# Issuing a pair's split, bits and spreading DMAs at the head of its period in a hashed attention and mixture-of-experts kernel

## The chip, the cores and the metric

The kernel runs on one NeuronCore of one Trainium2 chip. The metric is the device time of one execution in microseconds (us), the median of several runs. An execution profiled by the hardware gives the trace from which all rows below are read.

## The reference

Attention with a hash mask, then a mixture of eight experts of which each token uses one. Shapes: batch 4, 8 heads, 768 positions, head size 64; 3072 tokens of width 512 in the second part.

```python
q_bits = (einsum('bhsd,dk->bhsk', q, proj) > 0)      # 6 bits, and the same for k
mask = q_bucket[:, :, :, None] == k_bucket[:, :, None, :]
scores = where(mask, scale * q @ k.T, -1e9)
attn = softmax(scores)                               # + 1e-9 in the denominator
x = (attn @ v), heads side by side                   # 3072 x 512
e = argmax(x @ w_gate); gate = softmax(x @ w_gate)[e] * sigmoid(x @ w_output_gate)[e]
out = gate * relu(x @ w1[e]) @ w2[e]
```

## The kernel before

The first 480 us are attention, the rest experts; the change touches the attention alone. Two heads make a **pair** (16 pairs, `g`), and each pair takes 12 **steps** (`s`), one for a block of 128 queries of one head j. A step is a row of work on four engines: `scores(s)` on TensorE (PE, four matmuls into one of two `ps_s` buffers), `sc` on VectorE (DVE, line 533, reads `ps_s` and so frees it), `soft(s)` on ScalarE (ACT, the exponential, line 541), `normal` for two steps at a time (DVE: `rsum`, lines 548 and 549; GpSimd, POOL: two multiplications by it, line 551), and six steps later `transposed` (PE, line 562, and the ACT copies of line 563). Every sixth step (`k == 0`, k is s mod 6) has a **block of weighted sums** on PE (line 573, 12 matmuls in both heads) with its copy to `ot` on DVE (line 576) and the transposition `xb` (line 585). So the attention is a chain of **half periods** of six steps, each with one block; a pair has a first and a second half. In the trace a half period is read from the start of one block to that of the next.

Beside this, each pair g from 2 on is prepared one pair ahead, from step s0 = 12 (g - 1) on:

- `load(g)`: the two `qk` tiles from HBM, at step s0 - 5.
- `project(g)`: four matmuls behind the block at s0 (line 407), then the hash bits `bt` on DVE (line 410).
- `split_hi(g, j)`: the rounded part `xl` of head j, POOL, line 487, at s0 + 1 and s0 + 3.
- `split_lo(g, j, n)`: the rest `yl`, two halves for each head, DVE, line 495, at s0 + 3 to s0 + 6.
- `spread(g, j)`: eight DMAs in on-chip memory issued by the SP queue (lines 504 to 512), which place `xl`, `yl` and the bits in the operands of `scores`; at s0 + 4 and s0 + 6. The last two of them, line 512, put the query bits into `yl`.

The first step that uses all this for head 0 is s0 + 12, for head 1 it is s0 + 13. `xl`, `yl`, `xr` and `yr` have four buffers, so a pair's tiles take the place of those of two pairs before. In three of the pairs (steps 72, 120, 168) the DVE also works on the router's gate around s0 (lines 661 to 665 and 198 to 220, at step 168 with lines 767 to 776).

PE, DVE, ACT and POOL run in the order in which the code is written: the functions planned by `plan(step, ...)` come at the end of a step, those in `narrow` beside the block. The SP queue's order is set by a scheduler instead, and it is served strictly from the front: a DMA that waits holds all behind it.

## Time and profile before

| what | value |
|---|---|
| median of 3 runs | 816.14 us (815.57 to 816.91) |
| the profiled execution | 818.71 us, its span 816.9 us |
| PE busy | 767.9 us, 94% of the span |
| DVE, ACT, POOL busy | 489.1, 461.0 and 382.4 us |
| mean granted clock of PE | 0.971 of full speed |

Busy time is over the whole span; in a stretch of it another engine can be the one that is waited for. The 1.8 us between the profiled execution's time and its span lie outside the trace.

### The profile page before, as it was taken

To read this page: it belongs to the slowest core of one execution; us is meant where nothing else is said; L and a number is where in the kernel's file an instruction comes from. 1 tells how busy PE (TensorE), PEld (TensorE's weight loads), DVE (VectorE), ACT (ScalarE), POOL (GpSimd) and SP (SyncE) were. 2 spreads that over 40 slices of the span, in tenths; PEclk is the share of its full clock that TensorE was granted. 3 is DMA by queue.
4 is the path that set the end of the run, shared out by engine and by line. 5 is a ranking of instruction groups with operands and counts; after the bars stand their busy time and mean duration, and the time that the engine had idled before them with its cause. 6 is when DMAs were issued, how large, how long until landed. Compare 5 with 4: busy or idle time off the path is not lost. (4 is left out here: it accounts for less than half of the span.)

```text
span 816.9 us, 13705 instructions
## 1 busy us (share of the span) xinstructions
PE 767.9 (94%) x4690; PEld 619.9 (76%) x4690; DVE 489.1 (60%) x1032; ACT 461.0 (56%) x934; POOL 382.4 (47%) x422
## 2 busy tenths in 40 slices
PE   7999898999898999898998999979999999999997
PEld 5767566767656767667667767878899999998895
DVE  6778575788575788576777654434636354464740
ACT  6787575777675777676776873124333424253431
POOL 7456353444353444353435885443526463737201
PEclk8999998999998999999999999999999999999999
DMA  5545344456244455245345423435443545445511
GB/s 170 131 105 132 92 99 124 103 122 153 52 99 121 105 122 141 64 100 135 92 104 137 115 71 71 138 97 195 131 142 128 185 132 184 147 151 160 204 51 38
DMA packets 84798, 98.88 MB, mean 121 GB/s; under 512 B 57999, under 2 KB 59439, under 8 KB 84720
## 3 DMA queue, kind: packets, MB, share of 16 engines
q1 hardware_dynamic: 79376, 84.58, 38.9%
q0 software_dynamic: 5200, 13.31, 4.9%
q8 instruction: 40, 0.66, 0.3%
q14 instruction: 38, 0.31, 0.1%
q10 hardware_dynamic: 144, 0.02, 0.0%
HBM read 59.49 MB, written 13.11 MB: 89 GB/s over the span
## 5 line engine op out<-in xcount | busy, mean ns | idle before, releaser
L551 POOL TENSOR_SCALAR sc<-sc,rsum 128x768 f32<-128x768 f32 x192 | 176.7, 934 | 242.2 <-DVE rsum L549 146.7
L563 ACT COPY pts<-ps_t 128x384 f32<-128x384 f32 x384 | 165.8, 482 | 124.7 <-PE ps_t L562 124.3
L533 DVE TENSOR_SCALAR_CACHE_REDUCE sc<-ps_s 128x768 f32<-128x768 f32 x192 | 182.4, 954 | 79.3 <-PE ps_s L529 78.3
L541 ACT ACTIVATE sc<-sc,mn 128x768 f32<-128x768 f32 x192 | 178.7, 936 | 12.2 <-DVE sc L533 11.1
L562 PE MATMUL ps_t<-ident,sc 128*128 128x128 f32 x1152 | 168.9, 285 | 9.3 <-ACT pts L563 4.8
L562 PEld LDWEIGHTS ps_t<-ident,sc 128*128 128x128 f32 x1152 | 138.6, 146 | 45.0 <-POOL sc L551 20.9
L573 PE MATMUL ps_a<-pts,vt 128*64 128x384 f32 x768 | 131.9, 493 | 0.0
L529 PE MATMUL ps_s<-yr,yl 76*128 76x384 f32 x384 | 105.3, 357 | 23.7 <-DMA yl<-bt 23.0
L529 PE MATMUL ps_s<-xr,xl 128*128 128x384 f32 x384 | 119.6, 394 | 3.7 <-POOL xl L477 2.2
L573 PEld LDWEIGHTS ps_a<-pts,vt 128*64 128x64 f32 x768 | 52.5, 137 | 68.4 <-issue 68.2
L323 DVE SCALAR_TENSOR_TENSOR hl<-ps_s,hh 128x256 fp32r<-128x256 f32 (+8 forms) x40 | 34.0, 849 | 116.4 <-ACT hh L322 108.4
L312 PE MATMUL ps_s<-xh,w1h 128*128 128x256 f32 (+7 forms) x288 | 97.0, 337 | 0.0
L312 PE MATMUL ps_s<-xlo,w1h 128*128 128x256 f32 (+7 forms) x288 | 95.3, 331 | 0.0
L312 PE MATMUL ps_s<-xh,w1l 128*128 128x256 f32 (+7 forms) x288 | 95.1, 330 | 0.0
L529 PEld LDWEIGHTS ps_s<-yr,yl 76*128 76x128 f32 x384 | 73.8, 201 | 26.3 <-DMA xr<-xl 15.3
L286 POOL DMA_INDIRECT xq<-x_dram,idx x75 | 81.6, 1089 | 23.1 <-issue 20.5
L329 POOL DMA_INDIRECT out_dram<-yo,sid x29 | 30.5, 1052 | 123.3 <-ACT yo L328 72.3
L322 ACT ACTIVATE hh<-ps_s 128x256 fp32r<-128x256 f32 (+8 forms) x40 | 29.1, 727 | 104.3 <-PE ps_s L312 76.3
L529 PEld LDWEIGHTS ps_s<-xr,xl 128*128 128x128 f32 x384 | 61.5, 201 | 6.7 <-DVE sc L533 2.6
L312 PEld LDWEIGHTS ps_s<-xh,w1h 128*128 128x128 f32 x288 | 54.1, 188 | 2.1 <-issue 0.6
L312 PEld LDWEIGHTS ps_s<-xlo,w1h 128*128 128x128 f32 x288 | 54.1, 188 | 1.3 <-DVE xlo L269 0.2
L312 PEld LDWEIGHTS ps_s<-xh,w1l 128*128 128x128 f32 x288 | 54.1, 188 | 1.1
(204 smaller groups left out, 1034.5 us busy)
## 6 DMA issues: line engine op xcount, KB each, us to landing
w_raw<-in_w_dram SPq DMA_DIRECT2D x36, 512.0 KB
qk<-in_qkT_dram SPq DMA_DIRECT2D x32, 384.0 KB
xh<-in_w_dram SPq DMA_DIRECT2D x14, 512.0 KB
xlo<-in_w_dram SPq DMA_DIRECT2D x14, 512.0 KB
vt<-in_v_dram SPq DMA_DIRECT2D x16, 384.0 KB
xr<-xl SPq DMA_DIRECT2D x30, 192.0 KB
yr<-xl SPq DMA_DIRECT2D x30, 192.0 KB
xr<-yl SPq DMA_DIRECT2D x30, 192.0 KB
```

The costliest lines, as they stand in the source:

```text
L286: nc.gpsimd.indirect_dma_start(out=xq[:, k * P:(k + 1) * P], out_offset=None, in_=x_dram.rearrange("n (a f) -> (n a) f", a=NB32), in_offse ...
L312: nc.tensor.matmul(ps, l, r, start=first and k == 0, stop=last and k == len(pairs) - 1)
L322: nc.scalar.activation(hh, ph, AF.Relu)
L323: return lambda: nc.vector.scalar_tensor_tensor(hl, ph, 0.0, f32(hh), ALU.max, ALU.subtract)
L329: nc.gpsimd.indirect_dma_start(out=out[:, :], out_offset=bass.IndirectOffsetOnAxis(ap=sid[0:n, r, a:a + 1], axis=0), in_=yo[0:n], in_offse ...
L529: nc.tensor.matmul(ss[:, n, 0:HS], l[0:k, qs], r[0:k, n * HS:(n + 1) * HS], start=first, stop=not first)
L533: nc.vector.tensor_scalar(sc, ss[:, :, 0:HS], MASKED, None, ALU.min, ALU.min, accum_out=mn)
L541: nc.scalar.activation(pr, pr, AF.Exp, bias=mn, scale=-1.0, accum_out=sums[s // GROUP][:, k:k + 1])
L551: nc.gpsimd.tensor_scalar(live[s0 + k], live[s0 + k], rs[:, k:k + 1], 0.0, ALU.mult, ALU.add)
L562: nc.tensor.transpose(tr[:, c], pr[:, (3 * h + c) * P:(3 * h + c + 1) * P], ident)
L563: nc.scalar.copy(pts[:, 3 * h:3 * h + 3, t * P:(t + 1) * P], tr)
L573: nc.tensor.matmul(st["av"][j * D:(j + 1) * D], st["v"][:, j, c], blocks[hb][j][:, c], start=(c == 0), stop=(c == NT - 1))
```

## The change

For pairs from 2 on, the whole preparation is written at step s0 itself: both `split_hi` ahead of everything else there, the four `split_lo` in two groups behind the two `normals()` that follow the exponentials, then the block and `project`, then both `spread`. The loads come at s0 - 8. One of the six exponentials of a half period comes at k = 2 instead of k = 1. Pair 1 gets its own, slightly shifted steps. No instruction is added or removed, and no buffer changes.

```diff
--- before.py
+++ after.py
@@ -377,7 +377,7 @@
         batches = [dict() for _ in range(B)]
         blocks = {}
         sums = {}
-        at, narrow = {}, {}
+        at, first, amid, ahead, narrow, last = {}, {}, {}, {}, {}, {}
 
 
         LAG = PER
@@ -717,19 +717,21 @@
         for g in range(NP):
             s0 = 12 * (g - 1)
             if g >= 2:
-                plan(s0 - 5, lambda g=g: load(g))
+                plan(s0 - 8, lambda g=g: load(g))
+                first.setdefault(s0, []).extend(lambda g=g, j=j: split_hi(g, j) for j in range(2))
+                amid.setdefault(s0, []).extend(lambda g=g, n=n: split_lo(g, 0, n) for n in range(2))
+                ahead.setdefault(s0, []).extend(lambda g=g, n=n: split_lo(g, 1, n) for n in range(2))
+                narrow.setdefault(s0, []).append(lambda g=g: project(g))
+                last.setdefault(s0, []).extend(lambda g=g, j=j: spread(g, j) for j in range(2))
+            elif g == 1:
+                plan(4, lambda: project(1))
+                for j in range(2):
+                    plan(2 + j, lambda j=j: split_hi(1, j))
+                    for n in range(2):
+                        plan(3 + 2 * j + n, lambda j=j, n=n: split_lo(1, j, n))
+                    plan(5 + j, lambda j=j: spread(1, j))
             if g >= 1:
-                s0 += g == 1
-                if g == 1:
-                    plan(s0 + 4, lambda g=g: project(g))
-                else:
-                    narrow.setdefault(s0, []).append(lambda g=g: project(g))
                 plan(s0 + 10, lambda g=g: load_v(g))
-                for j in range(2):
-                    plan(s0 + 1 + 2 * j, lambda g=g, j=j: split_hi(g, j))
-                    for n in range(2):
-                        plan(s0 + 3 + 2 * j + n, lambda g=g, j=j, n=n: split_lo(g, j, n))
-                    plan(s0 + 4 + 2 * j, lambda g=g, j=j: spread(g, j))
             for hf in range(2 if g + 1 < NP else 1):
                 narrow.setdefault(12 * g + 6 * hf + 2 * PER, []).extend(
                     lambda hb=2 * g + hf, c=c: weighted(hb, c) for c in range(NT))
@@ -888,18 +890,23 @@
                     normals()
                     softs(1)
                 elif k == 0:
+                    for fn in first.get(s, ()):
+                        fn()
                     normals()
-                    while raw and raw[0] < s:
-                        softs(2)
-                        normals()
-                    for fn in narrow.get(s, ()):
+                    softs(2)
+                    normals()
+                    for fn in amid.get(s, ()):
                         fn()
-                    softs(1)
+                    softs(2)
+                    normals()
+                    for when in (ahead, narrow, last):
+                        for fn in when.get(s, ()):
+                            fn()
                 elif k == 3:
                     normals()
                 if s >= LAG:
                     transposed(s - LAG, live.pop(s - LAG))
-                if s >= PER and k in (1, 3):
+                if s >= PER and k in (2, 3):
                     softs(1)
                 for fn in at.get(s, ()):
                     fn()
```

On the SP queue the order of the DMAs changes with the code. Before, between the pair whose tiles are numbered below 1030 and the next one (from 1235 on); `xl`, `yl` and `bt` are sources or targets in on-chip memory:

```order
L506 DMA xr_1027<-yl_971 64x768
L507 DMA xl_920<-xl_920 64x768
L504 DMA xr_1302<-xl_1235 64x768
L512 DMA yl_971<-bt_835 12x384 x2
L505 DMA yr_1303<-xl_1235 64x768
L511 DMA yr_1303<-bt_1195 12x384 x2
```

After, the end of one pair's second `spread` (1163, 1182, 1208) and the beginning of the next pair's (1507, 1554):

```order
L512 DMA yl_1182<-bt_1205 12x384
L511 DMA yr_1208<-bt_1205 12x384
L512 DMA yl_1182<-bt_1205 12x384
L394 DMA qk_1325<-in_qkT_dram 128x768
L394 DMA qk_1327<-in_qkT_dram 128x768
L592 DMA x_dram_63<-xb_1239 32x24x32 x4
L399 DMA vt_1479<-in_v_dram 128x768
L504 DMA xr_1553<-xl_1507 64x768
L505 DMA yr_1554<-xl_1507 64x768
```

Before, the last two DMAs of a pair (line 512, `yl_971`) stand behind the next pair's line 504, which reads that pair's `xl_1235`. After, a pair's DMAs all stand ahead of the next pair's.

On DVE, from the `sc` of the step s0 (the third of the first row) to the steps after it, before:

```order
L533 TENSOR_SCALAR sc,mn<-ps_s 128x768 x3
L548 TENSOR_SCALAR rsum<-rsum 128x2
L549 RECIPROCAL rsum<-rsum 128x2
L548 TENSOR_SCALAR rsum<-rsum 128x2
L549 RECIPROCAL rsum<-rsum 128x2
L576 COPY ot<-ps_a 128x384
L410 TENSOR_SCALAR bt<-ps_m,pj 128x384
L585 STREAM_TRANSPOSE xb<-ot 128x384
L533 TENSOR_SCALAR sc,mn<-ps_s 128x768 x3
```

and after, at the same place:

```order
L533 TENSOR_SCALAR sc,mn<-ps_s 128x768 x3
L548 TENSOR_SCALAR rsum<-rsum 128x2
L549 RECIPROCAL rsum<-rsum 128x2
L495 SCALAR_TENSOR_TENSOR yl<-qk,pj,xl 128x384 x2
L548 TENSOR_SCALAR rsum<-rsum 128x2
L549 RECIPROCAL rsum<-rsum 128x2
L495 SCALAR_TENSOR_TENSOR yl<-qk,pj,xl 128x384 x2
L576 COPY ot<-ps_a 128x384
L410 TENSOR_SCALAR bt<-ps_m,pj 128x384
L585 STREAM_TRANSPOSE xb<-ot 128x384
L533 TENSOR_SCALAR sc,mn<-ps_s 128x768 x3
```

The four `split_lo` (line 495), which stood one by one between later `sc`, now all stand ahead of the `sc` of step s0 + 1. On POOL the two `split_hi` of a pair, before one by one with two multiplications of line 551 between them, now stand together ahead of those of s0:

```order
L487 TENSOR_SCALAR xl<-qk,pj 128x768 x2
L551 TENSOR_SCALAR sc<-sc,rsum 128x768 x10
```

## Rows read from the trace of the kernel before

**Rows 1.** The page's part 1: busy time of each engine, its share of the span, and the number of instructions.

```profile
PE 767.9 (94%) x4690; PEld 619.9 (76%) x4690; DVE 489.1 (60%) x1032; ACT 461.0 (56%) x934; POOL 382.4 (47%) x422
```

**Rows 2.** The view of waits, whole kernel, TensorE: who waited for whom, us in total, times, longest.

```profile
PE ps_s L529 <- DMA yl<-bt: 23.0, 7, 4.0
```

**Rows 3.** The same view for the SP queue, its largest row.

```profile
SPq L504 <- POOL xl L487: 105.9, 17, 10.1
```

**Rows 4.** The timeline at the first of these waits: start, us, engine, line, operation; in brackets the idle time before it and what ended it. The block at 83.75 us is that of step 36, and the bits in `bt` that line 512 moves are those of the pair whose scores PE is at.

```profile
82.03 1.47 SPq L507 DMA_DIRECT2D xl<-xl  x1
...
90.02 0.91 POOL L487 TENSOR_SCALAR xl<-qk,pj 128x768 fp32r<-128x768 f32 x1
90.95 0.46 SPq L504 DMA_DIRECT2D xr<-xl  x1
91.50 1.61 SPq L512 DMA_DIRECT2D yl<-bt  x2
...
93.79 0.98 PE L529 MATMUL ps_s<-yr,yl 76*128 76x384 f32 x2 [4.01 <-DMA yl<-bt]
```

**Rows 5.** Busy time by stretch, for six half periods from block to block: the stretch, its length, then busy us (and instructions) of PE, PE's weight loads, DVE, ACT and POOL, then the granted clock of PE, the share of the DMA engines and GB/s. First, second, first, second half of two pairs; a first half; and the first half from step 72, with the gate's work.

```profile
57.13:70.53 13.40, 13.40 (x93) 9.54 (x93) 9.90 (x22) 10.48 (x25) 7.97 (x12) 1.00 0.23 45
70.53:83.75 13.22, 12.68 (x86) 9.39 (x85) 10.26 (x24) 10.56 (x25) 7.46 (x22) 1.00 0.81 193
83.75:102.83 19.08, 15.07 (x93) 11.02 (x92) 9.74 (x22) 10.67 (x25) 7.49 (x13) 0.91 0.30 80
102.83:115.44 12.61, 12.61 (x86) 9.39 (x85) 9.99 (x24) 10.48 (x25) 6.38 (x7) 1.00 0.72 160
115.44:136.10 20.66, 17.30 (x102) 12.57 (x101) 10.77 (x24) 11.55 (x27) 7.66 (x8) 0.83 0.22 63
177.65:193.63 15.98, 14.92 (x105) 10.98 (x104) 14.12 (x35) 10.59 (x25) 7.74 (x8) 1.00 0.26 63
```

**Rows 6.** The timeline of the head of an undisturbed first half: the block, what DVE and POOL do beside it, the `sc` of step s0 + 1 (at 63.65), and PE's scores of step s0 + 3 (at 65.29).

```profile
57.13 4.09 PE L573 MATMUL ps_a<-pts,vt 128*64 128x384 f32 x24
57.33 0.96 DVE L533 TENSOR_SCALAR_CACHE_REDUCE sc<-ps_s 128x768 f32<-128x768 f32 x1 [0.53 <-PE ps_s L529]
...
58.21 0.16 DVE L548 TENSOR_SCALAR rsum<-rsum 128x2 f32<-128x2 f32 x1
...
58.77 1.79 POOL L551 TENSOR_SCALAR sc<-sc,rsum 128x768 f32<-128x768 f32 x2 [2.88 <-DVE rsum L549]
...
59.86 0.73 DVE L548 TENSOR_SCALAR rsum<-rsum 128x2 f32<-128x2 f32 x1 [1.28 <-ACT sc L541]
...
60.98 1.80 POOL L551 TENSOR_SCALAR sc<-sc,rsum 128x768 f32<-128x768 f32 x2 [0.42 <-DVE rsum L549]
...
61.27 0.56 DVE L576 COPY ot<-ps_a 128x384 f32<-128x384 f32 x1 [0.48 <-PE ps_a L573]
...
62.07 0.68 DVE L410 TENSOR_SCALAR bt<-ps_m,pj 128x384 fp32r<-128x384 f32 x1 [0.25 <-PE ps_m L407]
...
62.66 0.57 DVE L585 STREAM_TRANSPOSE xb<-ot 128x384 f32<-128x384 f32 x1
...
63.65 0.96 DVE L533 TENSOR_SCALAR_CACHE_REDUCE sc<-ps_s 128x768 f32<-128x768 f32 x1 [0.42 <-PE ps_s L529]
...
65.29 0.60 PE L529 MATMUL ps_s<-xr,xl 128*128 128x384 f32 x2
```

**Rows 7.** The timeline of the same half, later: two `split_lo` (line 495) on DVE beside two multiplications on POOL.

```profile
67.53 0.61 DVE L495 SCALAR_TENSOR_TENSOR yl<-qk,pj,xl 128x384 fp32r<-128x384 f32 x1
...
67.81 2.00 POOL L551 TENSOR_SCALAR sc<-sc,rsum 128x768 f32<-128x768 f32 x2 [3.24 <-PE ps_s L529]
68.06 0.95 DVE L533 TENSOR_SCALAR_CACHE_REDUCE sc<-ps_s 128x768 f32<-128x768 f32 x1
...
68.94 1.28 DVE L495 SCALAR_TENSOR_TENSOR yl<-qk,pj,xl 128x384 fp32r<-128x384 f32 x1
...
70.14 0.94 DVE L533 TENSOR_SCALAR_CACHE_REDUCE sc<-ps_s 128x768 f32<-128x768 f32 x1
```

**Rows 8.** The timeline of the first half from step 72 (block at 177.65 us): a gate operation, the `ot` copy, the `sc` of step s0 + 1, and PE's scores of step s0 + 3.

```profile
176.52 0.77 DVE L661 TENSOR_SCALAR den<-den 128x6 f32<-128x6 f32 x1
...
181.79 0.56 DVE L576 COPY ot<-ps_a 128x384 f32<-128x384 f32 x1 [1.03 <-PE ps_a L573]
...
185.58 0.94 DVE L533 TENSOR_SCALAR_CACHE_REDUCE sc<-ps_s 128x768 f32<-128x768 f32 x1
...
186.58 0.62 PE L529 MATMUL ps_s<-xr,xl 128*128 128x384 f32 x2 [0.52 <-DVE sc L533]
```

**Rows 9.** Two shorter waits of PE in the timeline, in the first halves from step 60 and from step 156, which have the same work.

```profile
162.77 0.85 PE L562 MATMUL ps_t<-ident,sc 128*128 128x128 f32 x6 [0.95 <-POOL sc L551]
...
407.36 1.12 PE L562 MATMUL ps_t<-ident,sc 128*128 128x128 f32 x6 [1.92 <-POOL xl L487]
```

**Rows 10.** These two half periods in the view by stretch, with the columns of rows 5.

```profile
149.67:164.25 14.58, 13.63 (x99) 9.93 (x96) 10.41 (x27) 10.42 (x27) 7.75 (x8) 1.00 0.27 64
393.30:409.70 16.40, 14.48 (x100) 10.60 (x96) 11.52 (x27) 11.14 (x27) 7.44 (x8) 0.94 0.31 71
```

**Rows 11.** The timeline of a second half (block at 70.53 us): a left-over `split_lo` and the wait of PE behind it.

```profile
75.76 1.21 DVE L495 SCALAR_TENSOR_TENSOR yl<-qk,pj,xl 128x384 fp32r<-128x384 f32 x1
...
79.42 0.84 PE L562 MATMUL ps_t<-ident,sc 128*128 128x128 f32 x6 [0.54 <-ACT pts L563]
```

## The prediction

> **What bounds the kernel now.** I read the busy times first: TensorE is busy 94% of the span [rows 1], so only what it waits for, or runs slowly through, can be won. The view of its waits comes next. Its one large row with a cause in the operands is a DMA: seven waits for `yl<-bt`, 23.0 us, the longest 4.0 [rows 2]. To see why these transfers are late I read the SP queue's own waits: it stood 105.9 us at line 504 for POOL's `xl` [rows 3]. The timeline joins the two [rows 4]. SP has issued line 507 by 83.5 us and then issues nothing until POOL has rounded the next pair's `xl` (90.02 to 90.93). It goes on with line 504 at 90.95 and only then with line 512, which moves bits that have been ready for half a period; PE, at the second step of this pair, starts its second product at 93.79, after 4.01 us of nothing. The reader is to see a queue served from the front: the transfer that PE needs stands behind one that belongs to the next pair. From issue to use it took under 2.3 us; what was late is the issue.
>
> The half periods give the price [rows 5]. An undisturbed first half takes 13.40 us, all of it PE busy. The disturbed one takes 19.08, 5.68 more, of which the wait is 4.01. The other 1.67 is the clock: its granted mean is 0.91, so for part of the stretch PE ran at 1.2 instead of 2.4 GHz, after the wait. A second one takes 20.66 at 0.83.
>
> **What the change removes.** In the new order of the SP queue a pair's line 512 always precedes the next pair's line 504, and both `spread` are issued a whole pair ahead. So the seven waits go: -23.0. With them goes the slow clock. For the first that is 1.67; for the second 20.66 - 13.40 - 3.4 = 3.9 (its wait, read as the mean of the seven, 23.0 / 7 = 3.3, moves this by 0.1). I take five of the first kind and two of the second, a choice: 5 x 1.7 + 2 x 3.9 = 16.3. Removed: -39.3 (all seven of the first kind would be -34.9).
>
> The half from step 156 holds a wait of 1.92 us at POOL [rows 9] and takes 16.40 where the same work takes 14.58 [rows 10]; a `split_hi` and a `split_lo` stand in that knot and go: -1.8.
>
> Second halves: 13.22 us where a `split_lo` is left over from the first half, 12.61 where none is [rows 5]; the 1.21 us of that instruction delay an exponential, then PE by 0.54 [rows 11]. No such remainder is left after the change. Against that, the exponential moved from k = 1 to k = 2 stands directly before that of k = 3, which makes ACT's copies late; I allow 0.2 us a half for it, less than half of that 0.54. About seven second halves win 0.4, seven lose 0.2: -1.4.
>
> The loads come earlier by three steps and land long before use; nothing waits for them: 0.
>
> **What it adds.** The moved work has the cover of a block (4.09 us) and of `project`. POOL's two `split_hi`, 0.91 each, fit in its 2.88 us of idle time before the first multiplication [rows 4, 6]: 0, and with that cover gone they would delay `rsum`'s readers by at most 1.8. DVE is the question, since the first `sc` after the block, that of step s0 + 1, frees the `ps_s` buffer for PE's scores of s0 + 3, and four `split_lo` now stand ahead of it. Before, DVE idles 1.28 + 0.48 + 0.25 + 0.42 = 2.4 us in this stretch, and the `sc` ends at 64.61, 0.7 before PE wants the buffer (65.29) [rows 6]. Together 3.1 us of cover against 4 x 0.61 = 2.4 [rows 7]. On these numbers the splits are free.
>
> They are not quite free, because of POOL. A `split_lo` that meets a running multiplication takes 1.28 instead of 0.61: begun at 68.94, it ends at 70.22, 0.41 after POOL's end at 69.81; and POOL's pair beside the earlier split takes 2.00 instead of 1.79 [rows 6, 7]. So the two take turns, instruction by instruction. `rsum` at 59.86 does the same: 0.73, until POOL's end. Walking the new order through the head, in us from the block's start: `rsum` 1.08, first split 1.36, POOL's first multiplication from 1.85 to 2.75, second split done 3.15, POOL's second to 4.05, second `rsum` 4.08, third split 4.15 to 4.7, POOL's third to 5.55, fourth split done 5.95, `ot` at 5.87 (before 4.14), `bt` 6.4, `xb` 7.0, `sc` from 7.5 to 8.45. PE wants the buffer at 8.16: a wait of 0.35. This walk lets an instruction start some 0.08 before the recorded end of the one ahead, as DVE does in rows 7; with full durations it gives 9.1, a wait of 1.0. I take 0.6 for each of the eleven heads without gate work: +6.6, with bounds 0 and 1.0 (11.0).
>
> The Trainium skill (GPSIMD Engine Reference, section 1, Specifications) says that POOL shares its SBUF interfaces with VectorE, with contention where a DVE instruction has two SBUF inputs or a two-port mode. `split_lo` has two such inputs, so by that rule the new place, beside POOL's four multiplications, is a bad one; the trace agrees (1.28 against 0.61 [rows 7]). If by that rule all four splits were to take 1.28, they would need 5.1 us against 3.1 of cover, a wait of 2.0 a head.
>
> In the three heads with gate work DVE has no slack: 14.12 us busy of 15.98 [rows 5], and PE already waits 0.52 for this same `sc` [rows 8]. The shift of `ot` alone (1.7) comes out as PE's wait. The small gate operations also meet POOL's `split_hi`, which now run just then (the one at 176.52 takes 0.77, waiting for POOL); two such meetings, each a little under the 0.9 of one POOL instruction, add about 1.5. That is 3.2 us of new wait and, since a wait of 1.92 was already followed by slower matmuls (granted clock 0.94 [rows 9, 10]), 1.7 for the clock: +4.9 each, +14.7. Bounds: 1.7 each, the shift alone, and 7.1, with the slow clock of the second kind (5.1 to 21.3 together).
>
> **The sum**, made against the profiled execution of 818.7: -39.3 - 1.8 - 1.4 + 6.6 + 14.7 = -21.2. That execution lies 2.6 above the median of the runs, and I take the difference as the same for both: 816.1 - 21.2 = 794.9, say **795**.
>
> **Rivals.**
> - DVE is not late. If the splits find POOL idle or go ahead of it, the wait is 0 in ordinary heads and the gate heads cost their lower bound: -42.5 + 5.1, about 779. For it: 3.1 us of cover against 2.4. Against it: the alternation in rows 7.
> - Slower: the new DVE wait lowers the clock at every head. A wait of 0.95 left the granted clock at 1.00, one of 1.92 did not [rows 9, 10], so it decides whether the wait comes out nearer 1.9. At 1.9 + 1.7 for eleven heads and 7.1 for three: -42.5 + 39.6 + 21.3 = +18.4, 834. It turns to a loss where the heads cost 42.5 / 14 = 3.0 each. The full 2.0 us wait of four colliding splits would lead here.
> - DVE somewhat later than my walk: 1.0 and 7.1: -42.5 + 11.0 + 21.3 = -10.2, 806.
> - The change does not do what it says, because the transfers themselves are slow or another one queues in front: about 816. Against it: landing took under 2.3 us from issue [rows 4], and the new queue has nothing of the next pair ahead.
>
> **How the numbers follow.** The likeliest, ordinary heads with a wait between 0.3 and 0.8, has 0.45 and gives 795, from 788 to 801. DVE in time 0.17 (779); DVE later 0.2 (801 to 814); slower 0.13; no effect 0.05. The range leaves out the part of the first rival below its centre and the slow one: 778 to 814. A change under 0.2% (1.6 us) is about what a measurement of this kernel cannot tell from none. Faster by more than that: 0.45 + 0.17 + 0.2 and a little of the last, 0.83; the same 0.04; slower 0.13.
>
> **What would show it.** The row `PE ps_s <- DMA yl<-bt` is gone and SP's waits at line 504 end before the block or stand for `split_hi` a whole pair ahead. First halves without gate work all take 13.5 to 14.5, with a short wait of PE for DVE's `sc` at s0 + 3; those from steps 72, 120 and 168 grow to some 20. The granted clock is 1.00 in ordinary halves. I am wrong if PE shows no wait at s0 + 3, if the ordinary halves fall below 1.00 in clock, or if another stretch (the first 30 us, the experts) moves by more than 2 us.

## The result, and the profile after

The changed kernel takes 788.31 us (median of 4, 785.37 to 789.06) where the kernel before takes 815.86 beside it: a ratio of 0.965, with a 95% interval from 0.963 to 0.968. That is 27.6 us less, and 6.7 below the forecast of 795. The profiled execution took 785.37, the shortest of the four, with a span of 783.7. The other three show a mean granted clock of PE of 0.984 to 0.986, the profiled one 0.990, which matters below.

Busy time (part 1 of the page after, which answers rows 1): PE is busy 14.3 us less with the same 4690 matmuls, of which fewer run at the lower clock (mean granted clock 0.990 against 0.971). The rest of the 33.3 us of span, 19.0, is idle time that is gone.

```profile
PE 753.6 (96%) x4690; PEld 608.5 (78%) x4690; DVE 494.7 (63%) x1032; ACT 459.2 (59%) x934; POOL 389.9 (50%) x422
```

PE's waits after, in the attention (the first 480 us): who waited for whom, us in total, times, longest. The row of [rows 2] is gone. The largest is now the wait for DVE's `sc`, which was 1.3 us in three waits before and is 12.4 in four.

```profile
PE ps_s L529 <- DVE sc L533: 12.4, 4, 4.0
PE ps_t L562 <- POOL sc L551: 1.7, 1, 1.7
```

The row of SP's waits in [rows 3] has fallen from 105.9 to 44.9:

```profile
SPq L504 <- POOL xl L487: 44.9, 13, 4.9
```

Three of those four waits in the timeline of PE, with the length of the matmuls behind them (the first of the four, 2.55 us, is at the start, under "Pair 1"):

```profile
178.10 0.62 PE L529 MATMUL ps_s<-xr,xl 128*128 128x384 f32 x2 [2.91 <-DVE sc L533]
...
290.09 1.01 PE L529 MATMUL ps_s<-xr,xl 128*128 128x384 f32 x2 [2.92 <-DVE sc L533]
...
405.80 1.01 PE L529 MATMUL ps_s<-xr,xl 128*128 128x384 f32 x2 [3.99 <-DVE sc L533]
```

And the half periods after, with the columns of [rows 5]: a first and a second half of an ordinary pair (the first is that of rows 6), the first half from step 60, and the three first halves with gate work (steps 72, 120, 168).

```profile
59.26:72.82 13.56, 13.44 (x94) 9.54 (x93) 11.71 (x25) 10.46 (x25) 8.63 (x14) 1.00 0.44 94
72.82:85.60 12.78, 12.66 (x85) 9.38 (x85) 8.32 (x20) 10.47 (x25) 7.05 (x20) 1.00 0.60 131
139.87:153.72 13.85, 13.63 (x100) 9.93 (x96) 11.92 (x28) 10.31 (x27) 6.80 (x7) 1.00 0.51 106
166.79:184.80 18.01, 14.98 (x106) 11.07 (x105) 16.01 (x37) 10.86 (x25) 7.96 (x8) 1.00 0.42 88
278.77:299.30 20.53, 17.61 (x105) 13.82 (x104) 16.12 (x37) 11.10 (x25) 7.97 (x8) 0.83 0.41 84
393.27:413.57 20.30, 16.31 (x105) 12.39 (x105) 17.15 (x44) 10.87 (x25) 7.98 (x8) 0.92 0.40 83
```

The first halves without gate work are even now: 13.57, or 14.35 where eight matmuls of the router's logits (0.78 us) stand in one, or 13.85 (steps 60, 108, 156), and each kind takes the same in every place, at a granted clock of 1.00. What is left lies in the three gate halves.

Added up, the spans tell where the 33.3 us are: up to the block of step 12 the kernel is 2.4 **longer** (32.91 against 30.51 us); from there to step 180 it is 31.4 shorter (393.91 against 425.32); from step 180 to the end 4.3 shorter, nearly all of it in the experts, which the change doesn't touch.

### The profile page after: what moved, and what is told of

The parts are those of the page before. It is cut to its first block, busy times and chain, and to the rows that moved or that the text cites. A ratio compares the mean times of both kernels' runs of the same rounds, so it can differ in the third digit from the quotient of the medians.

```text
span 783.7 us, 13717 instructions
## 1 busy us (share of the span) xinstructions
PE 753.6 (96%) x4690; PEld 608.5 (78%) x4690; DVE 494.7 (63%) x1032; ACT 459.2 (59%) x934; POOL 389.9 (50%) x422
## 5 line engine op out<-in xcount | busy, mean ns | idle before, releaser
L551 POOL TENSOR_SCALAR sc<-sc,rsum 128x768 f32<-128x768 f32 x192 | 189.0, 998 | 206.0 <-DVE rsum L549 128.8
L562 PE MATMUL ps_t<-ident,sc 128*128 128x128 f32 x1152 | 163.2, 278 | 5.9 <-POOL sc L551 1.7
L562 PEld LDWEIGHTS ps_t<-ident,sc 128*128 128x128 f32 x1152 | 132.8, 142 | 42.8 <-issue 20.2
L529 PE MATMUL ps_s<-xr,xl 128*128 128x384 f32 x384 | 116.5, 385 | 14.7 <-DVE sc L533 12.4
L529 PE MATMUL ps_s<-yr,yl 76*128 76x384 f32 x384 | 100.6, 343 | 0.4 <-POOL yr L439 0.3
L529 PEld LDWEIGHTS ps_s<-xr,xl 128*128 128x128 f32 x384 | 59.5, 195 | 17.0 <-DVE sc L533 14.4
L529 PEld LDWEIGHTS ps_s<-yr,yl 76*128 76x128 f32 x384 | 71.3, 192 | 1.0 <-POOL yr L439 1.0
L495 DVE SCALAR_TENSOR_TENSOR yl<-qk,pj,xl 128x384 fp32r<-128x384 f32 x60 | 57.6, 997 | 2.1 <-POOL xl L487 1.8
```

Source lines behind the costliest of these rows:

```text
L495: nc.vector.scalar_tensor_tensor(st["yl"][j][:, cs], st["qk"][j][:, cs], sgn, f32(st["xl"][j][:, cs]), ALU.mult, ALU.subtract)
L529: nc.tensor.matmul(ss[:, n, 0:HS], l[0:k, qs], r[0:k, n * HS:(n + 1) * HS], start=first, stop=not first)
L551: nc.gpsimd.tensor_scalar(live[s0 + k], live[s0 + k], rs[:, k:k + 1], 0.0, ALU.mult, ALU.add)
L562: nc.tensor.transpose(tr[:, c], pr[:, (3 * h + c) * P:(3 * h + c + 1) * P], ident)
```

## The experiments

They ask three questions: what made the seven waits, what the moved low parts cost, and what the small edits do.

### What made the waits: the queue's order, or the late split?

**Only SP's order.** In the kernel before, SP's DMAs go in the order in which they are written, instead of the scheduler's.

```diff
-        with tc.manual_schedule(engines=MANUAL):
+        with tc.manual_schedule(engines=MANUAL | {mybir.EngineType.SP}):
```

> The kernel before with one change: the SP queue of the attention is issued in the order in which the code is written, instead of the scheduler's order; all compute stays where it was. Theory Q (the queue: PE waits because line 512 stands behind the next pair's line 504): the row PE <- DMA yl<-bt goes from 23.0 us to under 1, all seven long first halves shrink to 13.4 to 14.6, the start of the first block stays at 30.5, the gate halves stay near 16, and the time falls by about 33 us to 783 (778 to 790). Rival P (the gain needs the splits inside the block's cover): the waits come back as waits for DVE's sc or POOL, and the time stays above 800.

Measured: 818.57 us, ratio 1.005 (1.002 to 1.008). No gain, so theory Q misses the time, though the seven waits are gone as it said; another row has taken their place, and it is not one that rival P named. The waits of PE in the attention:

```profile
PE ps_m L407 <- DMA qk<-in_qkT_dram: 27.7, 22, 2.9
```

The SP queue shows why (its largest row of waits, and the timeline around the block at 90.73 us):

```profile
SPq L506 <- DVE yl L495: 113.5, 15, 9.3
```

```profile
92.36 0.71 SPq L512 DMA_DIRECT2D yl<-bt  x1
93.12 0.98 SPq L394 DMA_DIRECT2D qk<-in_qkT_dram  x2
```

and PE, in the same stretch:

```profile
96.53 0.84 PE L407 MATMUL ps_m<-qk,pjc 128*32 128x384 f32 x4 [1.72 <-DMA qk<-in_qkT_dram]
```

In program order the loads of q and k stand behind the second `spread` of the pair, eight DMAs of which line 506 waits for DVE's low parts. The loads are issued at 93.12, and `project` wants them at 94.8. The half takes 16.15 us. It is the same fault with another victim: what PE needs soon stands behind what waits. The order alone moves the wait, it doesn't remove it.

**SP's order and earlier loads.** The same, and one number more:

```diff
-                plan(s0 - 5, lambda g=g: load(g))
+                plan(s0 - 8, lambda g=g: load(g))
```

> The kernel before, with SP's queue in program order (as in the first experiment) and the loads three steps up, nothing else of the change: splits, bits and spreading where they were. In the first experiment the waits for yl<-bt were gone, but PE then waited 27.7 us, 22 times, for the loads of q and k at line 407, because these had come to stand in the queue behind the second spread of the pair (issued at 93.12, behind line 512 at 92.36). Theory Q (the queue's order is all: what PE waits for stands behind something that waits): three steps up they stand ahead of the second spread, the 27.7 us go and nothing takes their place: 815.3 - 27.7 = 788, from 784 to 794, without a single instruction of DVE or POOL moved. Theory H (the early split is needed as such, since the split that comes late would hold any order of the queue): the waits come back at ps_s for xr or yr, 805 or more.

Measured: 779.37 us, ratio 0.951 (0.947 to 0.956), **better than the changed kernel**, with every instruction of DVE and POOL where it was. The loads come out in the middle of the queue's period, ahead of the second `spread`:

```profile
76.21 0.71 SPq L512 DMA_DIRECT2D yl<-bt  x1
76.98 0.97 SPq L394 DMA_DIRECT2D qk<-in_qkT_dram  x2
...
81.75 0.54 SPq L504 DMA_DIRECT2D xr<-xl  x1
```

No half from step 12 on shows a granted clock under 1.00 any more before the end of the attention, and the gate halves are as short as the best of before [rows 5] (first half of an ordinary pair, then step 72; step 120 takes 15.97):

```profile
84.94:98.32 13.38, 13.38 (x93) 9.53 (x92) 9.88 (x22) 10.46 (x25) 7.61 (x13) 1.00 0.47 106
...
167.34:183.30 15.96, 14.93 (x105) 10.99 (x104) 14.10 (x35) 10.57 (x25) 7.71 (x8) 1.00 0.33 77
```

So the prediction's reading of the cause stands, and theory H, that the late split would hold any order, falls. Earlier loads in the scheduler's order, with nothing else, were not run; that they are not what removes the waits for `yl<-bt` is seen in the first experiment, where these waits went with the loads at their old step.

**Only the early `split_hi`.** In the kernel before, both `split_hi` at the head of the period; SP's order stays the scheduler's.

```diff
-                    plan(s0 + 1 + 2 * j, lambda g=g, j=j: split_hi(g, j))
+                    if g == 1:
+                        plan(s0 + 1 + 2 * j, lambda g=g, j=j: split_hi(g, j))
+                    else:
+                        first.setdefault(s0, []).append(lambda g=g, j=j: split_hi(g, j))
...
                 elif k == 0:
+                    for fn in first.get(s, ()):
+                        fn()
                     normals()
```

> The kernel before with one edit: both split_hi of a pair from the second on are issued at the head of its period, as in the changed kernel; low parts, spreading, loads, exponentials, pair 1 and the kind of SP's order stay. Theory Q: what held SP at line 504 was the time of split_hi, so the seven waits for yl<-bt (23.0) and the slow clock after them (16.3) go: 816.9 - 39 = 778 at best, 780 to 790 with some waits left over. Theory L (the earlier loads are needed for it): split_hi at the head meets loads that have not landed, POOL stands, its multiplications and so PE come late: 795 or more.

Measured: 784.23 us, ratio 0.956 (0.951 to 0.960). One wait of the seven remains (3.3 us, at step 168, in a half of 20.53 with a granted clock of 0.83), the others are gone. Line 504 still stands ahead of line 512, and SP still waits there, but 41.5 us instead of 105.9 and at most 4.6: in the half from step 36 line 512 is issued 0.28 us after the block's start, where in the kernel before it was 7.76.

The wait that remains has another cause, and had it in the kernel before. There SP stands 6.6 us at line 763, where it reads the number of the expert whose weights are loaded early. DVE works that number out behind the gate (the view names `base`, which it writes right after), and line 512 stands in the queue behind it. In this run the same stand (line 766 of its kernel) takes 8.0 us. The row of SP's waits before, its queue and PE's wait:

```profile
SPq L763 <- DVE base L776: 6.6, 1, 6.6
```

```profile
419.17 0.59 SPq L507 DMA_DIRECT2D xl<-xl  x1
427.28 0.39 SPq L168 DMA_DIRECT2D w_raw<-in_w_dram  x1
...
431.87 0.98 PE L529 MATMUL ps_s<-yr,yl 76*128 76x384 f32 x2 [2.36 <-DMA yl<-bt]
```

So six of the seven waits stood behind line 504, one behind the gate's work on DVE. By the ratios this one edit gives more than the whole change (0.956 against 0.965). The old distance of the loads does no harm here, so theory L falls.

**The low parts and the spreading back.** The changed kernel, with `split_lo` and `spread` at their old steps.

```diff
-                amid.setdefault(s0, []).extend(lambda g=g, n=n: split_lo(g, 0, n) for n in range(2))
-                ahead.setdefault(s0, []).extend(lambda g=g, n=n: split_lo(g, 1, n) for n in range(2))
-                last.setdefault(s0, []).extend(lambda g=g, j=j: spread(g, j) for j in range(2))
+                for j in range(2):
+                    for n in range(2):
+                        plan(s0 + 3 + 2 * j + n, lambda g=g, j=j, n=n: split_lo(g, j, n))
+                    plan(s0 + 4 + 2 * j, lambda g=g, j=j: spread(g, j))
```

> The changed kernel with split_lo and spread back at their old steps (s0 + 3 to s0 + 6); split_hi stays at the head and the loads stay early. The SP order again has the next pair's line 504 ahead of this pair's line 512. Theory Q in its form 'what holds the queue is how late split_hi comes': split_hi is done near the start of the block, 5 us before PE needs the bits, so the wait row is under 2 us all the same; 780 to 790, and the gate waits of 2.9, 2.9 and 4.0 us are under 1.5 each since DVE has only split_hi's contention. Rival O (the order itself is what costs): 7 or more waits for yl<-bt, over 15 us together, 800 or more.

Measured: 785.86 us, ratio 0.962 (0.959 to 0.964). The halves from steps 72 and 120 fall from 18.01 and 20.53 to 15.74 and 15.72. The third doesn't (20.16): with the `spread` at its old steps it has the stand of the kernel before, 8.3 us for the expert's number, then the load of its weights (line 168) and behind it line 512. PE waits 3.74 for that. It is the only wait for the bits, so rival O falls, though the row is not under the 2 us of theory Q.

```profile
384.64 0.59 SPq L507 DMA_DIRECT2D xl<-xl  x1
394.51 0.39 SPq L168 DMA_DIRECT2D w_raw<-in_w_dram  x1
395.01 1.67 SPq L512 DMA_DIRECT2D yl<-bt  x2
```

```profile
SPq L766 <- DVE base L779: 8.3, 1, 8.3
```

### What the moved low parts cost

**One split more, and two.** The changed kernel with a dose: the last `split_lo` of each head done once or twice more, into the same place.

```diff
+                ahead[s0].append(lambda g=g: split_lo(g, 1, 1))
```

For two more, in the same place:

```diff
+                ahead[s0].extend(lambda g=g: split_lo(g, 1, 1) for n in range(2))
```

> The changed kernel with one more split_lo on DVE in each head (the last of the four done twice into the same place, same values): a dose of 0.6 to 1.3 us of DVE ahead of the first sc after the block. Read from the changed kernel's trace, that sc ends 0.23 us before PE wants its buffer. Theory S (0.23 is the true slack and DVE's chain is serial here): PE waits 0.4 to 1.0 in each of 11 ordinary heads and 0.6 to 1.3 more in the three with gate work: +6 to +15, 794 to 803. Theory N (DVE has more cover than that, since splits that come later meet no POOL work): under 2 us more, 786 to 790.

> As the run with one more split_lo in each head, with two more. Theory S: PE waits 1.0 to 2.3 in each head; a wait of 1.9 has lowered the clock and one of 0.95 has not, so the cost rises faster than the dose: +14 to +40, 802 to 828. Theory N: under 6 us more, below 794.

Measured: 799.28 and 807.65 us, ratios 0.974 (0.970 to 0.979) and 0.985 (0.981 to 0.989). Both times lie in the band of theory S. PE's wait for `sc` in an ordinary half, with one split more and then with two:

```profile
70.92 0.62 PE L529 MATMUL ps_s<-xr,xl 128*128 128x384 f32 x2 [0.85 <-DVE sc L533]
```

```profile
71.99 0.62 PE L529 MATMUL ps_s<-xr,xl 128*128 128x384 f32 x2 [1.50 <-DVE sc L533]
```

None, 0.85, 1.50: in eight of the eleven ordinary heads the first split more costs PE a wait of 0.75 to 0.87 and the second another 0.65, all of it on the path. So the changed kernel stands right at the edge there; DVE has no hidden cover. In the three heads from steps 60, 108 and 156 the `sc` is done earlier (7.39 us after the block's start, where PE wants it at 8.49), and there the first split costs nothing (13.84 against 13.85); theory S had a wait in all eleven. The clock stayed at 1.00 in these halves, even after the wait of 1.50 (second kernel, by stretch):

```profile
62.08:77.12 15.04, 13.54 (x94) 9.65 (x93) 13.49 (x27) 10.69 (x25) 8.87 (x14) 1.00 0.37 79
```

**The gate's work four steps later.** The changed kernel, with the last gate operations moved away from the heads at 72, 120 and 168.

```diff
-                          (21, r["gate_sums"]), (22, r["gate_values"]), (22, r["places"]), (24, r["columns"]),
-                          (25, r["hot"]), (28, r["table"]), (29, r["entries"])):
+                          (21, r["gate_sums"]), (26, r["gate_values"]), (26, r["places"]), (27, r["columns"]),
+                          (28, r["hot"]), (29, r["table"]), (30, r["entries"])):
```

> The changed kernel with the gate's work of three pairs moved past the head: gate values and places from k = 4 of the half before to k = 2, the columns from k = 0 to k = 3, hot to k = 4, table to k = 5, entries one step on. If the three long waits for DVE's sc (2.9, 2.9, 4.0 us) come from that work standing ahead of it together with the splits, they fall under 1 us each, the three halves from 18.0, 20.5 and 20.3 to 14 to 16, and the time by 8 to 14 us to 774 to 780. Rival: DVE is short in any place, the waits only move some steps on, and the time stays within 3 us of 788.

Measured: 783.06 us, ratio 0.960 (0.958 to 0.963), some 5 less than the changed kernel and between the two theories, neither of which is met. Its gate halves take 17.00, 17.86 and 18.62, not the 15.97 (steps 72 and 120) of the kernel that leaves the low parts alone: the moved operations have a new wait of PE, at line 226, and at step 120 a lower clock (0.95) that goes on in the second half (13.48 instead of 12.78).

```profile
PE ps_m L226 <- DVE t_ob L220: 5.6, 3, 2.0
```

So part of the gate halves' price was this collision of low parts and gate work; moving the gate's work took away a part of that price, not all of it.

### The small edits

**Pair 1.** The changed kernel with pair 1's steps as before.

```diff
-                plan(4, lambda: project(1))
+                plan(5, lambda: project(1))
+                plan(11, lambda: load_v(1))
-                    plan(2 + j, lambda j=j: split_hi(1, j))
+                    plan(2 + 2 * j, lambda j=j: split_hi(1, j))
-                        plan(3 + 2 * j + n, lambda j=j, n=n: split_lo(1, j, n))
-                    plan(5 + j, lambda j=j: spread(1, j))
+                        plan(4 + 2 * j + n, lambda j=j, n=n: split_lo(1, j, n))
+                    plan(5 + 2 * j, lambda j=j: spread(1, j))
-            if g >= 1:
+            if g >= 2:
```

> The changed kernel with the steps of pair 1 put back to where they were before (split_hi, split_lo, spread, project and load_v one or two steps later). Theory P (their shift is what made the start longer, 32.91 against 30.51 us to the block of step 12: in the trace PE waits 2.55 for DVE's sc at 19.99 and 1.68 for POOL's sc at 25.54): the block of step 12 is back at 30.2 to 30.8, the time at 785 to 787. Rival (the start varies by itself, or the earlier loads make it longer): 32 to 33, and 788.

Measured: 784.09 us, ratio 0.962 (0.959 to 0.964); the block of step 12 starts at 30.86, within 0.4 of before and 0.06 past the band of theory P; the time is a little under it. The intervals of this ratio and of the changed kernel's (0.963 to 0.968) overlap, so it is the traces that tell: the block of step 12 starts at 30.2 to 31.9 in the seven kernels with pair 1's old steps, and at 32.9 to 34.6 in the six with the new ones. Earlier loads alone don't make it late: this kernel has them. Two waits are gone that the changed kernel has there (the changed kernel's PE timeline):

```profile
19.99 1.01 PE L529 MATMUL ps_s<-xr,xl 128*128 128x384 f32 x2 [2.55 <-DVE sc L533]
...
25.54 0.85 PE L562 MATMUL ps_t<-ident,sc 128*128 128x128 f32 x6 [1.68 <-POOL sc L551]
```

Their cause stands in the changed kernel's DVE timeline: the first `split_lo` is queued ahead of an `sc` and waits 1.76 us for POOL's `split_hi`.

```profile
17.80 1.25 DVE L495 SCALAR_TENSOR_TENSOR yl<-qk,pj,xl 128x384 fp32r<-128x384 f32 x1 [1.76 <-POOL xl L487]
18.98 0.94 DVE L533 TENSOR_SCALAR_CACHE_REDUCE sc<-ps_s 128x768 f32<-128x768 f32 x1
```

**Gate and pair 1 together.** The changed kernel with both edits above.

> As e3_gate, and with pair 1's preparation back at the steps that it had before the change. If the late start (first block at 32.91 instead of 30.51 us) comes from pair 1's two split_hi in a row, which the first split_lo waits for, the first block starts at 30.5 again and the time is 2.4 us (1.5 to 3.5) under e3_gate's. Rival: the time is won at the start and lost at the next block, no difference.

Measured: 780.54 us, ratio 0.957 (0.954 to 0.961). One execution of the five took 4193 us, and the trace is of that one; it is not read here, so this kernel is known by its other times only. The two gains nearly add up: by the ratios 0.0052 and 0.0037 apart, 0.0080 together, which with intervals of some 0.003 on either side is no more than agreement. That the first block starts at 30.5 again was not seen.

**The exponentials.** The changed kernel with them at k = 1 and 3 again.

```diff
-                if s >= PER and k in (2, 3):
+                if s >= PER and k in (1, 3):
```

> The changed kernel with the exponentials back at k = 1 and 3 instead of 2 and 3. The kernel with the early split_hi alone has both halves at 13.39 and 13.18, the one with the low parts at their old steps but the exponentials at k = 2 and 3 has 13.57 and 12.79, and in the kernel before a second half without a left-over split_lo took 12.61 [rows 5]. Theory T (the left-over split costs 0.6 in the second half; the move of the exponentials costs 0.2 in each half and was a remedy for that split alone): halves of 13.38 and 12.61, so 0.36 less a pair, 783 to 785. Rival (the move of the exponentials is what shortens the second half): 13.38 and 13.2, 0.25 more a pair, 790 to 793.

Measured: 789.00 us, ratio 0.968 (0.965 to 0.971), not to be told from the changed kernel. Both theories miss. The second half is the 12.61 of theory T, but the first is 13.92 and not 13.38. Its halves by stretch, and the wait in the first:

```profile
60.71:74.63 13.92, 13.44 (x94) 9.54 (x93) 11.72 (x25) 10.55 (x25) 8.79 (x14) 1.00 0.45 96
74.63:87.24 12.61, 12.61 (x86) 9.38 (x85) 8.33 (x20) 10.46 (x25) 6.89 (x20) 1.00 0.58 128
```

```profile
68.75 0.94 ACT L541 ACTIVATE sc<-sc,mn 128x768 f32<-128x768 f32 x1 [0.44 <-DVE sc L533]
...
70.29 0.85 PE L562 MATMUL ps_t<-ident,sc 128*128 128x128 f32 x6 [0.48 <-ACT pts L563]
```

The exponential at k = 1 needs the `sc` of step s0 + 1, the one that now stands behind the four splits: ACT waits 0.44 for it, then its copies come late, then PE. In the kernel with SP's order and earlier loads the same exponential stands at k = 1, that `sc` is done half a microsecond earlier, and the first half takes 13.38. So at k = 2 the exponential costs 0.18 in a first half, and at k = 1 behind the moved splits 0.43 to 0.54.

**The best of it.** SP in program order, loads three steps up, exponentials at k = 2 and 3; splits, spreading and pair 1 as before. Then the same with `split_hi` at the head as well.

> The kernel with SP in program order and the loads three steps up (779.4), and the exponentials at k = 2 and 3. Here the splits stay at their old steps, so the left-over split_lo is there. By the halves of the run with the low parts at their old steps (13.57 and 12.79 against 13.38 and 13.21): 0.24 less a pair, some 3 us, 776. If the move of the exponentials costs 0.2 in each half whatever stands there: 0.4 more a pair, 784.

> The kernel before with SP in program order, loads three steps up, exponentials at k = 2 and 3, and split_hi at the head of the period with project behind the block; low parts, spreading and pair 1 at their old steps. It differs from the run of the same call without the early split only in split_hi. Theory Q (the place of split_hi matters only through SP's queue): with the queue in program order nothing is left to win, within 2 us of that run, 774 to 778. Rival (an early split_hi has a worth of its own, by freeing POOL later in the period): 3 us or more below it. Rival (it costs, since POOL's two instructions now stand ahead of the multiplications): 3 us or more above it.

Measured: **774.82 us**, ratio 0.950 (0.948 to 0.953), and 775.79, ratio 0.951 (0.948 to 0.954). The first is near the 776 that was expected, and far from the 784. By the ratio it can't be told from the kernel without the moved exponentials (0.951); the halves show the gain, 0.24 a pair. With the queue in program order the early `split_hi` is worth nothing more: its place mattered through the queue alone. The first of the two is 9.3 below the changed kernel with the old pair 1 (784.09), measured beside it. Its halves (an ordinary pair; step 72; step 120 takes the same 15.64):

```profile
57.41:70.97 13.56, 13.44 (x93) 9.53 (x93) 10.07 (x22) 10.46 (x25) 8.10 (x12) 1.00 0.39 89
70.97:83.75 12.78, 12.66 (x85) 9.37 (x85) 9.81 (x24) 10.46 (x25) 7.29 (x22) 1.00 0.60 137
167.04:182.68 15.64, 15.01 (x105) 11.10 (x104) 14.12 (x35) 10.69 (x25) 7.73 (x8) 1.00 0.29 71
```

These ordinary halves equal those of the changed kernel, which so owes nothing to its moved low parts there. The 12.78 of the second half shows more: here the left-over `split_lo` still stands in it, so the move of the exponential alone takes away what that split cost (13.20 without it). In the gate halves DVE is busy 14.1 us instead of 16.0, and they are 2.4 and 4.9 shorter, the clock of the second included.

## Why the prediction came out as it did

The direction, the range and, for six of the seven waits, the mechanism of the gain were right: the waits for `yl<-bt` went, and the run with SP's order and earlier loads shows their cause without moving an instruction of DVE or POOL. PE now waits for DVE's `sc` at s0 + 3, but only around the gate.

The price was not right, and two of the signs of being wrong that the prediction named came true: in ordinary heads PE shows no wait at s0 + 3, and two stretches that had no term moved by more than 2 us, the start (2.4) and the experts (4.3). The likeliest case, a wait of 0.3 to 0.8 in ordinary heads, did not occur; that 788.31 lies at the edge of its band (788 to 801) is luck. Between the profiled executions the span fell by 33.3 us where the sum said 21.2. In the medians it is 27.6, since the profiled execution of the kernel before lies 2.9 above its median and that of the changed kernel 2.9 below.

The terms, from the halves between steps 12 and 180, in us. Measured is the half of the changed kernel less that of before; where the half of before was a disturbed one, the difference is split at its undisturbed length, read from the kernel with SP's order and earlier loads:

| term | predicted | measured |
|---|---|---|
| seven waits and the slow clock | -39.3 | -36.5 |
| knot at step 156 | -1.8 | -1.8 |
| second halves | -1.4 | -3.4 |
| eleven ordinary heads | +6.6 | -0.8 |
| three gate heads | +14.7 | +11.1 |
| sum | -21.2 | -31.4 |
| start, to step 12 | 0 | +2.4 |
| from step 180 on | 0 | -4.3 |

**The seven waits.** Right but for 2.8 us. The half of 20.66 in [rows 5] was read as 13.40 of work, a wait, and 3.9 of slow clock. Its count of instructions, 102 against 93, was in the row: it holds the logits' matmuls, 0.78 us, and so do those from steps 96 and 144. Against its true undisturbed length (14.17) it lost 6.49, of which 3.36 is its wait and 3.1, not 3.9, the clock; the half from step 96 is alike. The rest is the seventh wait, at step 168: 2.36 us, with a granted clock of 0.91 in that half, and yet the half is only 2.8 longer than in the kernel with SP's order and earlier loads, where PE has a wait of 0.55 of its own. That wait also had another cause than the prediction gave it, SP's stand at line 763 and not at line 504 [rows 3]; it went because the new order has the bits a whole pair ahead.

**The ordinary heads** are the term that failed, by 7.4. The walk had the second `rsum` wait for POOL's second multiplication, until 4.08 us after the block's start. The timeline of DVE and POOL after, in the half whose block starts at 85.60:

```profile
87.53 1.26 DVE L495 SCALAR_TENSOR_TENSOR yl<-qk,pj,xl 128x384 fp32r<-128x384 f32 x1
88.71 0.16 DVE L548 TENSOR_SCALAR rsum<-rsum 128x2 f32<-128x2 f32 x1
...
89.89 1.26 DVE L495 SCALAR_TENSOR_TENSOR yl<-qk,pj,xl 128x384 fp32r<-128x384 f32 x1
...
92.61 0.92 DVE L533 TENSOR_SCALAR_CACHE_REDUCE sc<-ps_s 128x768 f32<-128x768 f32 x1
```

```profile
87.21 4.70 POOL L551 TENSOR_SCALAR sc<-sc,rsum 128x768 f32<-128x768 f32 x4 [0.64 <-DVE rsum L549]
...
88.36 1.20 POOL L551 TENSOR_SCALAR sc<-sc,rsum 128x768 f32<-128x768 f32 x1
```

`rsum` begins at 3.11 after the block's start, directly behind the second split (87.53) and within POOL's second multiplication (88.36 to 89.56), and takes 0.16. All behind it comes earlier; `sc` is done at 7.93 where PE wants the buffer at 8.16. The walk had 8.45. Up to that `rsum` its steps were right (first two splits done at 3.15, measured 3.19), and the splits did take turns with POOL as the walk had it. What failed is the step from the 0.73 of [rows 6] to every `rsum` beside POOL. In the trace before, all 28 `rsum` of the attention that begin within an instruction of POOL (lines 487 and 551) end with it, and so do 17 after; but the 14 that follow a split directly take 0.16, all of them. No `rsum` that met POOL stood directly behind a split before, so [rows 6] could not show it; why the order matters stays open. A slack of 0.23 decided over 6.6 us of forecast, which is why the rival "DVE is not late" (779) should have had more than its 0.17; its zero for the ordinary heads came true, its 1.7 for each gate head did not. Eight of the heads cost some 0.18 all the same, the price of the moved exponential: the kernels with that move and the old place of the low parts have the same 13.57. The prediction had this 0.2 a half, but its sum counts it in second halves alone. The three heads from steps 60, 108 and 156 gained 0.73 each (14.58 to 13.85), since the splits left a place where POOL's `sc` was late [rows 9, 10]; with the low parts back at their old steps they take 14.57 again. That was not seen in advance.

**The gate heads** were forecast as 3.2 of wait and 1.7 of clock each. The wait grew by 2.4 (0.52 to 2.91) at the first two, and the halves by 2.0 and 4.5: the clock cost nothing at step 72 and 2.5 us at step 120, after a wait that differs by 0.01. Of the three profiled executions with these waits, the changed kernel, that with pair 1 back and that with the exponentials back, the half from step 72 has a granted clock of 1.00 in two (18.0 us) and of 0.83 in the third (20.48). In the other executions of the changed kernel the mean clock is lower and the span 2.1 to 3.6 longer, which fits a fall at step 72 there too; without their traces this is argued, not shown.

**The second halves** were counted wrongly: of the fourteen, nine gained (0.16 to 0.71), three stood still and two lost 0.18, where seven and seven were assumed. The largest gain, 0.71 at step 162, holds a lower clock of before (0.95). And the gain is not owed to the left-over `split_lo` being gone: the best kernel has the same 12.78 with that split in it.

**The start** got no term, although the diff shifts pair 1: an error of omission. The same walk through DVE's order would have shown a `split_lo` ahead of `sc`, waiting for POOL. The run with pair 1's old steps shows what stood in its place.

**The experts**, nearly all of the 4.3 from step 180 on, hold one large difference: in the kernel before PE waits there 3.8 us for ACT's `hh`, and ACT had been idle for 10.48 until a release that the view only calls remote; slower matmuls follow.

```profile
547.54 0.60 ACT L322 ACTIVATE hh<-ps_s 128x512 fp32r<-128x512 f32 x1 [10.48 <-remote]
...
548.19 0.80 PE L312 MATMUL ps_m<-w2h,hh 128*128 128x512 f32 x1 [3.80 <-ACT hh L322]
```

The kernels with the early `split_hi` alone, and with the low parts put back, have it too (2.3 and 2.1 us) and take 361 us from step 180 to the end; the others take 355 to 358. Each kernel has one trace, so it stays open whether the program or the single execution makes this wait, and why; no run was made for it.

## What to carry to other kernels

Where a queue is served from the front, read what stands ahead of the late transfer, for each late transfer by itself (here six stood behind one line and the seventh behind another), and then ask the same of every transfer in the new order: program order for SP alone moved the wait from the bits to the loads, and three steps on one line then won some 40 us without touching an engine. Move work between busy engines only after the order of the queue has been tried: here the moved low parts won 0.7 us in three halves and cost 2.0 to 4.5 in three others, and the queue's order with earlier loads and one moved exponential came out some 9 us lower without them. When a forecast hangs on a slack of a few tenths of a microsecond, give both outcomes like chances; count the instructions of a stretch before calling its length a disturbance.

## What the runs showed of the hardware

A wait of the same length is not always followed by a lower clock. In the changed kernel PE's next matmuls took 0.62 after a wait of 2.91 us (granted clock 1.00 over that half) and 1.01 after one of 2.92 (0.83). With two splits more they took 0.62 after 1.50 (1.00). Nor is the longer wait the slower one: in the kernel before, the half with the wait of 2.36 at step 168 has a granted clock of 0.91.

DVE and POOL slow each other. In the head after, read one by one, the four splits take 0.62, 1.26, 0.89 and 1.26 us. The first begins before POOL's multiplications; each of the others ends 0.40 to 0.41 after the end of the multiplication within which it began, as the 1.28 of [rows 7] did. POOL's four take 1.17 to 1.20 each, where one takes 0.91 in [rows 6]. Together the splits take 4.02, between the 2.4 and the 5.1 that the prediction had as its two ends. An `rsum` of 128x2 that finds POOL at work ends with POOL's instruction, unless it follows a split directly: then it takes 0.16 (14 of 14). The Trainium skill (GPSIMD Engine Reference, section 1, Specifications) states that POOL's SBUF interfaces are shared with VectorE, with contention where a DVE instruction has two SBUF inputs; for the splits, which have two, the trace agrees.

The SP queue is served from the front here, whatever it waits for. It stood for a POOL result (105.9 us at line 504), for DVE's low parts (113.5 us at line 506 in program order) and for a number that it reads itself (6.6 us at line 763), and each time transfers that PE needed were issued only after it.
